# ScalarE's Softplus and Erf in place of exp, log, a polynomial and tanh in a feed-forward kernel

## Chip, cores and metric

The kernel runs on one core of a Trainium2 chip (trn2). The time is that of the device, in microseconds (us), from the core's start to its end; several executions are made and their median is given. Lower is better.

## What is computed

Two blocks follow each other. The first is attention between 512 tokens and 32 states of each of 8 heads, in both directions, for 8 batches; the second is a feed-forward block over all 8 * 544 = 4352 resulting rows, with an activation that is the input times the error function of its softplus:

```python
# x (8, 8, 512, 64), state (8, 8, 32, 64); softmax over the last axis, scale = 1/8
xread = softmax(scale * x @ state.T) @ state          # 512 rows per head
sread = softmax(scale * state @ x.T) @ x              # 32 rows per head
rows = concatenate([xread, sread], axis=2)            # -> (8 * 544, 512)
h = rows @ w_in                                       # w_in (512, 2048)
sp = maximum(h, 0) + log1p(exp(-abs(h)))              # softplus
out = (h * erf(sp)) @ w_out                           # w_out (2048, 512)
```

The two weights arrive as float64 and are made into float32 on the core.

## The kernel before

**Chunks and groups.** The feed-forward block goes over nine chunks of rows: one for the 512 token rows of each of the eight batches, and one for the 256 state rows of all batches together. A chunk is worked in four groups `g`; a group is four tiles of 128 hidden features. For each group `hidden` (line 239) makes the product with `w_in` (line 246: per tile four products over the 512 inputs, each run by TensorE as two MATMUL instructions on float32) into an accumulator tile `h` of PSUM, of which there are two (pool `ps_h`). ScalarE copies each tile into `hs` (line 248). The activation then runs over the whole group at once, 128 x 2048 elements for a chunk of 512 rows: VectorE cuts h at 3.95 (256), ScalarE takes exp (257), GpSimd adds one (258), ScalarE takes the logarithm (259), GpSimd makes the rounding's remainder in two steps (260, 261), VectorE subtracts it (262), ScalarE squares (263), VectorE runs a polynomial of degree 8 (264, six instructions at 267, 269), ScalarE takes tanh (271) and VectorE multiplies by `hs` (272). The result `gT` is the stationary operand of `project` (line 275), whose products with `w_out` (278) add up in four PSUM accumulators over the four groups. After the last group `store` copies them out on ScalarE (286) and SyncE's queue sends them to memory.

**Order.** The loop calls `hidden` of group g, then `project` of group g-1 (held back in `pending`), and after every odd group one of the two `attention` calls for the next batch. So between the hidden products of group g-1 and the projection of g-1 TensorE has the hidden products of group g to do. The four compute engines run their own queues in order; a planner that works from estimated durations makes those orders from the program, which is why the transposes of an attention stand between hidden products in the trace.

**Attention** (line 148) has a front part on TensorE: transposes of the state and of x (153, 161), and the two score products (169, 190). Then VectorE and ScalarE make the two softmaxes (175 to 202; exp on ScalarE at 179 and 198). The back part on TensorE is the transposes of the two results (206, 213), the products with the state (221) and with x (229). ScalarE copies each intermediate result out of PSUM. Two attentions run before the first chunk, and two during each of the first seven chunks.

**Weights.** During the first chunk each group first loads its two pieces of `w_in` and two of `w_out` (`weights`, line 134). A piece arrives as float64 bits in a buffer of the name `hs` (line 109; two buffers, shared with the `hs` of `hidden`), and seven instructions of VectorE (115 to 128; the last of them writes the weight tile) make it float32.

**Buffers** of the pool `act` (`hs`, `u`, `s`, `gT`) are two each; `w` is one.

Of the kernel before, what the change touches and what calls it, by code (L numbers as in the profile page):

```python
# [8 lines left out]
F32 = mybir.dt.float32  # L9
U32 = mybir.dt.uint32  # L10
ALU = mybir.AluOpType
ACTF = mybir.ActivationFunctionType
AX = mybir.AxisListType
PSUM = bass.MemoryType.PSUM

# erf(s) = tanh(s * P(s^2)) on 0 <= s <= 3.97, P of degree 8: its relative error is 3e-8, half a
# unit of fp32's last place. Above that erf is 1 in fp32; softplus(H_ONE) = 3.969, so h is cut there
# before it is made into s (and not where it multiplies the erf).
H_ONE = 3.95
ERF_P = [  # L20
    1.1283792021879724,
    0.10277131634542137,
    -0.0002021555576414212,
    -0.0006036769380557052,
    7.648746087340316e-05,
    -1.8604810636552222e-06,
    -5.151776104349058e-07,
    5.392234410610488e-08,
    -1.6409115403957545e-09,
]  # L30


@with_exitstack
def kernel(
# [8 lines left out]
    nc = tc.nc  # L43
    B, H, S, D = x.shape
    Ns = state.shape[2]
    d_model, d_ff = moe_w_in.shape
    P = 128
# [26 lines left out]

    # Rows (head of four, n), columns (head of the pair, d): each head's state in its own half, so
    # that a pair of heads is one product.
    st = const.tile([P, NH, B, 2 * D], F32, name="st")
# [3 lines left out]

    # Row p holds the tokens 4p .. 4p+3 of each head.
    def load_x(b, hb):
# [17 lines left out]
    def weight(dst, src, shape):  # L101
        """A piece of a weight. The bits of a float64 are made into a float32 here, rounded to
        the nearest."""
        if src.dtype == F32:
            nc.sync.dma_start(out=dst, in_=src)
            return
        i = shape[1]
        n = shape[0] * i
        raw = act.tile([P, 2 * n], U32, name="hs")
        nc.sync.dma_start(out=raw.rearrange("p (o i) -> p o i", i=2 * i), in_=src.bitcast(U32))  # L110
        words = raw.rearrange("p (n w) -> p n w", w=2)
        lo, hi = words[:, :, 0], words[:, :, 1]
        # 2^exponent with the sign: float32's bias is 896 less; what is too small becomes 0.
        e = act.tile([P, n], U32, name="u")
        nc.vector.tensor_scalar(e, hi, 20, 0x7FF, op0=ALU.logical_shift_right,
                                op1=ALU.bitwise_and)
        nc.vector.tensor_scalar(e, e, -896.0, 0.0, op0=ALU.add, op1=ALU.max)
        nc.vector.tensor_scalar(e, e, 255.0, 8388608.0, op0=ALU.min, op1=ALU.mult)
        nc.vector.scalar_tensor_tensor(out=e, in0=hi, scalar=0x80000000, in1=e,
                                       op0=ALU.bitwise_and, op1=ALU.bitwise_or)  # L120
        # The significand's upper 21 bits, and with the lower 32 behind the point.
        m = act.tile([P, n], U32, name="s")
        nc.vector.tensor_scalar(m, hi, 0xFFFFF, 0x100000, op0=ALU.bitwise_and,
                                op1=ALU.bitwise_or)
        f = act1.tile([P, n], F32, name="w")
        nc.vector.scalar_tensor_tensor(out=f, in0=lo, scalar=2.0 ** -32, in1=m,
                                       op0=ALU.mult, op1=ALU.add)
        nc.vector.scalar_tensor_tensor(  # L128
            out=dst, in0=f.rearrange("p (o i) -> p o i", i=i), scalar=2.0 ** -20,
            in1=e.bitcast(F32).rearrange("p (o i) -> p o i", i=i), op0=ALU.mult, op1=ALU.mult)  # L130
# [13 lines left out]

    # The state's own rows of the second part, features on the partitions, for all batches.
    sT = const.tile([P, NK, B, Ns], F32, name="sT")

    def attention(b, hb, xx):
        """Four heads of a batch: their rows of xx [feature, pair, token] and of sT."""
        xt = x_t.pop((b, hb))  # L150
# [13 lines left out]

        # Each token over the states.
        s1 = ps_at.tile([P, NC, QH, Ns], F32, name="at")
# [19 lines left out]

        # Each state over the tokens.
        s2 = ps_at.tile([P, S], F32, name="at")
# [35 lines left out]

        # Of each pair's product the blocks of one head with itself.
        sr = ps_at.tile([P, 2, 2 * Ns], F32, name="at")
# [8 lines left out]

    lead = ERF_P[-1]
    cs = [c / lead for c in ERF_P]

    def hidden(xx, n, g):
        """h * erf(softplus(h)) for four tiles of the hidden features, [feature, tile, token]."""  # L240
        hs = act.tile([P, GF, S], F32, name="hs")[:, :, 0:n]
        for i in range(GF):
            f0 = P * (GF * g + i)
            hp = ps_h.tile([P, S], F32, name="h")
            for k in range(NK):
                nc.tensor.matmul(out=hp[:, 0:n], lhsT=w_in[:, k, f0:f0 + P], rhs=xx[:, k, :],  # L246
                                 start=(k == 0), stop=(k == NK - 1))
            nc.scalar.copy(hs[:, i, :], hp[:, 0:n])  # L248

        # s = log1p(u) with u = exp(h): ln(w) - ((w - 1) - u), where w is 1 + u as it was rounded  # L250
        # and what follows it is exact, which keeps the small ones.
        u = act.tile([P, GF, S], F32, name="u")[:, :, 0:n]
        s = act.tile([P, GF, S], F32, name="s")[:, :, 0:n]
        w = act1.tile([P, GF, S], F32, name="w")[:, :, 0:n]
        gT = act.tile([P, GF, S], F32, name="gT")[:, :, 0:n]
        nc.vector.tensor_scalar(u, hs, H_ONE, None, op0=ALU.min)  # L256
        nc.scalar.activation(out=u, in_=u, func=ACTF.Exp)  # L257
        nc.gpsimd.tensor_scalar(w, u, 1.0, 1.0, op0=ALU.add, op1=ALU.mult)  # L258
        nc.scalar.activation(out=s, in_=w, func=ACTF.Ln)  # L259
        nc.gpsimd.tensor_scalar(w, w, -1.0, 1.0, op0=ALU.add, op1=ALU.mult)  # L260
        nc.gpsimd.tensor_tensor(w, w, u, op=ALU.subtract)  # L261
        nc.vector.tensor_tensor(s, s, w, op=ALU.subtract)  # L262
        nc.scalar.activation(out=u, in_=s, func=ACTF.Square)  # L263
        nc.vector.scalar_tensor_tensor(out=gT, in0=u, scalar=cs[-2], in1=u,  # L264
                                       op0=ALU.add, op1=ALU.mult)
        for c in cs[-3:0:-1]:
            nc.vector.scalar_tensor_tensor(out=gT, in0=gT, scalar=c, in1=u,  # L267
                                           op0=ALU.add, op1=ALU.mult)
        nc.vector.scalar_tensor_tensor(out=gT, in0=gT, scalar=cs[0], in1=s,  # L269
                                       op0=ALU.add, op1=ALU.mult)  # L270
        nc.scalar.activation(out=gT, in_=gT, func=ACTF.Tanh, scale=lead)  # L271
        nc.vector.tensor_tensor(gT, gT, hs, op=ALU.mult)  # L272
        return gT
# [90 lines left out]
```

## Time and profile before

| | |
|---|---|
| median of 3 runs | 1462.73 us (1460.02 to 1465.14) |
| span of the profiled execution, first to last instruction | 1459.6 us |
| TensorE (PE) busy | 1153.4 us, 79% |
| VectorE (DVE) busy | 1054.3 us, 72% |
| ScalarE (ACT) busy | 531.0 us, 36% |
| GpSimd (POOL) busy | 296.5 us, 20% |
| mean granted clock of TensorE | 0.889 of full speed |

The profile is of one execution on the chip. Its page lists, engine by engine, the busy time; the chain of work that ended last, followed back from the last instruction; and the groups of instructions with their idle time ahead of them and what ended that idle time. Ends of matmuls are modelled, so times between the starts of TensorE's instructions are more telling than the durations of single ones. "PEld" is TensorE's loading of the stationary operand, which runs beside the products. The granted clock is TensorE's, as a share of its full 2.4 GHz.

### The profile page before, as it was taken

What the parts mean: (1) busy time and instruction counts of PE and PEld (TensorE: products, weight loads), DVE (VectorE), ACT (ScalarE), POOL (GpSimd) and SP (SyncE); (2) the same over time, 40 slices, a digit from 0 to 9 for tenths busy, and PEclk for the clock granted to TensorE, in tenths of its full rate; (3) what the DMA queues carried; (4) which work ended last, traced back from release to release, by engine and by line L of the source; (5) the groups of instructions that cost most, each with busy time, mean ns of one, the idle gap of its engine ahead of it and who ended that gap; (6) DMA issues with size and microseconds to landing.
All of it is one profiled execution on the core that took longest, in us unless ns stands there. A gap on an engine that the chain in (4) does not pass through costs nothing.

```text
span 1459.6 us, 8120 instructions
## 1 busy us (share of the span) xinstructions
PE 1153.4 (79%) x3152; PEld 558.7 (38%) x3152; DVE 1054.3 (72%) x685; ACT 531.0 (36%) x587; POOL 296.5 (20%) x114
## 2 busy tenths in 40 slices
PE   6758575979897996979697969797897969694964
PEld 4434232434343443434343434343443424242541
DVE  2897988695758569495939585776858593859673
ACT  2323231434243343443344243434243334333432
POOL 0012020403222222222222221303022222222121
PEclk9968787979797998989798989999898979897987
DMA  4312221000000000000010001000000000000000
GB/s 129 101 44 86 88 71 58 15 29 0 15 0 29 15 1 11 33 0 15 0 44 0 15 0 29 15 15 0 0 29 0 0 0 29 0 0 0 29 0 15
DMA packets 45350, 35.13 MB, mean 24 GB/s; under 512 B 36864, under 2 KB 36864, under 8 KB 45312
## 3 DMA queue, kind: packets, MB, share of 16 engines
q1 hardware_dynamic: 45312, 34.61, 7.8%
q8 instruction: 25, 0.41, 0.1%
q14 instruction: 13, 0.11, 0.0%
HBM read 25.69 MB, written 8.91 MB: 24 GB/s over the span
## 4 chain that ended last, share of the span: by engine, by line
DVE 39%; PE 29%; ACT 16%; POOL 13%; issue 2%; DMA 0%; SPq 0%; POOLq 0%; ACTq 0%
DVE gT L267 18%; PE o L278 15%; PE h L246 9%; POOL w L261 7%; DVE gT L272 5%; ACT s L259 4%; ACT u L257 4%; POOL w L258 4%; DVE s L262 4%; DVE gT L264 3%; POOL w L260 3%; DVE u L256 3%; ACT u L263 3%; ACT gT L271 2%; PE at L229 2%
## 5 line engine op out<-in xcount | busy, mean ns | idle before, releaser
L278 PE MATMUL o<-w_out,gT 128*128 128x512 f32 x1088 | 510.9, 630 | 189.9 <-DVE gT L272 189.7
L246 PE MATMUL h<-xx,w_in 128*128 128x512 f32 x1024 | 467.9, 610 | 53.1 <-DVE w_in L128 52.8
L267 DVE SCALAR_TENSOR_TENSOR gT<-gT,u 128x2048 f32<-128x2048 f32 (+1 forms) x216 | 479.2, 2219 | 5.9
L278 PEld LDWEIGHTS o<-w_out,gT 128*128 128x128 f32 x1088 | 218.4, 203 | 477.7 <-issue 268.1
L246 PEld LDWEIGHTS h<-xx,w_in 128*128 128x128 f32 x1024 | 196.1, 196 | 294.4 <-issue 236.3
L258 POOL TENSOR_SCALAR w<-u 128x2048 f32<-128x2048 f32 (+1 forms) x36 | 66.4, 1845 | 1057.2 <-ACT u L257 1057.2
L262 DVE TENSOR_TENSOR s<-s,w 128x2048 f32<-128x2048 f32 (+1 forms) x36 | 78.1, 2169 | 222.8 <-POOL w L261 222.8
L248 ACT COPY hs<-h 128x512 f32<-128x512 f32 (+1 forms) x144 | 79.1, 560 | 293.3 <-PE h L246 243.9
L261 POOL TENSOR_TENSOR w<-w,u 128x2048 f32<-128x2048 f32 (+1 forms) x36 | 162.6, 4518 | 3.0
L272 DVE TENSOR_TENSOR gT<-gT,hs 128x2048 f32<-128x2048 f32 (+1 forms) x36 | 109.8, 3051 | 56.4 <-ACT gT L271 56.4
L263 ACT ACTIVATE u<-s 128x2048 f32<-128x2048 f32 (+1 forms) x36 | 65.4, 1815 | 161.5 <-DVE s L262 161.5
L264 DVE SCALAR_TENSOR_TENSOR gT<-u 128x2048 f32<-128x2048 f32 (+1 forms) x36 | 78.2, 2172 | 36.3 <-ACT u L263 36.0
L271 ACT ACTIVATE gT<-gT 128x2048 f32<-128x2048 f32 (+1 forms) x36 | 65.4, 1816 | 106.4 <-DVE gT L269 106.3
L269 DVE SCALAR_TENSOR_TENSOR gT<-gT,s 128x2048 f32<-128x2048 f32 (+1 forms) x36 | 101.8, 2827 | 0.7
L257 ACT ACTIVATE u<-u 128x2048 f32<-128x2048 f32 (+1 forms) x36 | 65.4, 1816 | 60.3 <-DVE u L256 60.3
L260 POOL TENSOR_SCALAR w<-w 128x2048 f32<-128x2048 f32 (+1 forms) x36 | 66.8, 1854 | 72.9 <-ACT s L259 72.9
L259 ACT ACTIVATE s<-w 128x2048 f32<-128x2048 f32 (+1 forms) x36 | 65.4, 1815 | 20.7 <-POOL w L258 20.6
L256 DVE TENSOR_SCALAR u<-hs 128x2048 f32<-128x2048 f32 (+1 forms) x36 | 41.9, 1163 | 32.6 <-ACT hs L248 32.6
L209 ACT COPY aT<-at 128x512 f32<-128x512 f32 x16 | 9.4, 584 | 121.3 <-PE at L206 121.2
L259 ACT ACT_TABLE_LOAD x36 | 46.2, 1283 | 0.6
L169 PE MATMUL at<-stT,xT 128*128 128x64 f32 x256 | 39.5, 305 | 7.8 <-ACT xT L163 7.4
L229 PEld LDWEIGHTS at<-a2T,x 128*128 128x128 f32 x256 | 36.4, 226 | 23.1 <-ACT xx L223 22.6
(55 smaller groups left out, 617.6 us busy)
## 6 DMA issues: line engine op xcount, KB each, us to landing
x<-in_x_dram SPq DMA_DIRECT2D x64, 128.0 KB, 2.9
hs<-in_moe_w_in_dram SPq DMA_DIRECT2D x8, 1024.0 KB, 5.2
hs<-in_moe_w_out_dram SPq DMA_DIRECT2D x8, 1024.0 KB, 4.8
out_dram<-ot SPq DMA_DIRECT2D x32, 256.0 KB, 2.2
st<-in_state_dram SPq DMA_DIRECT2D x8, 64.0 KB, 2.2
out_dram<-ot SPq DMA_DIRECT2D x8, 64.0 KB, 1.7
```

The costliest lines, as they stand in the source:

```text
L246: nc.tensor.matmul(out=hp[:, 0:n], lhsT=w_in[:, k, f0:f0 + P], rhs=xx[:, k, :], start=(k == 0), stop=(k == NK - 1))
L257: nc.scalar.activation(out=u, in_=u, func=ACTF.Exp)
L258: nc.gpsimd.tensor_scalar(w, u, 1.0, 1.0, op0=ALU.add, op1=ALU.mult)
L259: nc.scalar.activation(out=s, in_=w, func=ACTF.Ln)
L260: nc.gpsimd.tensor_scalar(w, w, -1.0, 1.0, op0=ALU.add, op1=ALU.mult)
L261: nc.gpsimd.tensor_tensor(w, w, u, op=ALU.subtract)
L262: nc.vector.tensor_tensor(s, s, w, op=ALU.subtract)
L263: nc.scalar.activation(out=u, in_=s, func=ACTF.Square)
L264: nc.vector.scalar_tensor_tensor(out=gT, in0=u, scalar=cs[-2], in1=u, op0=ALU.add, op1=ALU.mult)
L267: nc.vector.scalar_tensor_tensor(out=gT, in0=gT, scalar=c, in1=u, op0=ALU.add, op1=ALU.mult)
L272: nc.vector.tensor_tensor(gT, gT, hs, op=ALU.mult)
L278: nc.tensor.matmul(out=acc[r], lhsT=gT[:, i, P * r:P * r + P], rhs=w_out[:, GF * g + i, :], start=(g == 0 and i == 0), stop=(g == NG - 1 a ...
```

## The change

Each tile of h is now read from its accumulator by two engines: ScalarE's Softplus writes `s`, and VectorE's copy writes `hs`. When the four tiles of a group are there, one Erf of ScalarE runs over all of them in place, and VectorE multiplies by `hs`. The cut at 3.95, exp, logarithm, the three GpSimd instructions, the square, the polynomial and tanh are gone, with their constants; nothing is left for GpSimd in the loop. Everything outside `hidden` is as it was (comments fell away, so line numbers move).

```diff
     def hidden(xx, n, g):
         hs = act.tile([P, GF, S], F32, name="hs")[:, :, 0:n]
+        s = act.tile([P, GF, S], F32, name="s")[:, :, 0:n]
+        gT = act.tile([P, GF, S], F32, name="gT")[:, :, 0:n]
         for i in range(GF):
             f0 = P * (GF * g + i)
             hp = ps_h.tile([P, S], F32, name="h")
             for k in range(NK):
                 nc.tensor.matmul(out=hp[:, 0:n], lhsT=w_in[:, k, f0:f0 + P], rhs=xx[:, k, :],
                                  start=(k == 0), stop=(k == NK - 1))
-            nc.scalar.copy(hs[:, i, :], hp[:, 0:n])
-
-        u = act.tile([P, GF, S], F32, name="u")[:, :, 0:n]
-        s = act.tile([P, GF, S], F32, name="s")[:, :, 0:n]
-        w = act1.tile([P, GF, S], F32, name="w")[:, :, 0:n]
-        gT = act.tile([P, GF, S], F32, name="gT")[:, :, 0:n]
-        nc.vector.tensor_scalar(u, hs, H_ONE, None, op0=ALU.min)
-        nc.scalar.activation(out=u, in_=u, func=ACTF.Exp)
-        nc.gpsimd.tensor_scalar(w, u, 1.0, 1.0, op0=ALU.add, op1=ALU.mult)
-        nc.scalar.activation(out=s, in_=w, func=ACTF.Ln)
-        nc.gpsimd.tensor_scalar(w, w, -1.0, 1.0, op0=ALU.add, op1=ALU.mult)
-        nc.gpsimd.tensor_tensor(w, w, u, op=ALU.subtract)
-        nc.vector.tensor_tensor(s, s, w, op=ALU.subtract)
-        nc.scalar.activation(out=u, in_=s, func=ACTF.Square)
-        nc.vector.scalar_tensor_tensor(out=gT, in0=u, scalar=cs[-2], in1=u,
-                                       op0=ALU.add, op1=ALU.mult)
-        for c in cs[-3:0:-1]:
-            nc.vector.scalar_tensor_tensor(out=gT, in0=gT, scalar=c, in1=u,
-                                           op0=ALU.add, op1=ALU.mult)
-        nc.vector.scalar_tensor_tensor(out=gT, in0=gT, scalar=cs[0], in1=s,
-                                       op0=ALU.add, op1=ALU.mult)
-        nc.scalar.activation(out=gT, in_=gT, func=ACTF.Tanh, scale=lead)
-        nc.vector.tensor_tensor(gT, gT, hs, op=ALU.mult)
+            nc.scalar.activation(out=s[:, i, :], in_=hp[:, 0:n], func=ACTF.Softplus)
+            nc.vector.tensor_copy(hs[:, i, :], hp[:, 0:n])
+        nc.scalar.activation(out=s, in_=s, func=ACTF.Erf)
+        nc.vector.tensor_tensor(gT, s, hs, op=ALU.mult)
         return gT
```

## Rows read from the trace of the kernel before

**Rows 1.** The page's part 1: busy time (share of the span) and number of instructions
```profile
PE 1153.4 (79%) x3152; PEld 558.7 (38%) x3152; DVE 1054.3 (72%) x685; ACT 531.0 (36%) x587; POOL 296.5 (20%) x114
```

**Rows 2.** The page's part 4: the chain that ended last, by engine and line
```profile
DVE 39%; PE 29%; ACT 16%; POOL 13%; issue 2%; DMA 0%; SPq 0%; POOLq 0%; ACTq 0%
DVE gT L267 18%; PE o L278 15%; PE h L246 9%; POOL w L261 7%; DVE gT L272 5%; ACT s L259 4%; ACT u L257 4%; POOL w L258 4%; DVE s L262 4%; DVE gT L264 3%; POOL w L260 3%; DVE u L256 3%; ACT u L263 3%; ACT gT L271 2%; PE at L229 2%
```

**Rows 3.** Costliest groups, shapes merged: busy, mean ns of one | idle before, releaser
```profile
L278 PE MATMUL o<-w_out,gT 128*128 128x512 f32 x1088 | 510.9, 630 | 189.9 <-DVE gT L272 189.7
L246 PE MATMUL h<-xx,w_in 128*128 128x512 f32 x1024 | 467.9, 610 | 53.1 <-DVE w_in L128 52.8
L267 DVE SCALAR_TENSOR_TENSOR gT<-gT,u 128x2048 f32<-128x2048 f32 (+1 forms) x216 | 479.2, 2219 | 5.9
...
L248 ACT COPY hs<-h 128x512 f32<-128x512 f32 (+1 forms) x144 | 79.1, 560 | 293.3 <-PE h L246 243.9
```

**Rows 4.** TensorE's timeline, two groups and one attention: start, us, instructions [idle before]
```profile
731.25 0.60 PE L206 MATMUL at<-ident,a 128*128 128x128 f32 x4
...
732.53 1.61 PE L221 MATMUL at<-aT,st 64*128 64x512 f32 x4 [0.24 <-ACT aT L209]
734.32 2.00 PE L229 MATMUL at<-a2T,x 128*128 128x64 f32 x16 [0.19 <-ACT xx L223]
736.16 10.52 PE L246 MATMUL h<-xx,w_in 128*128 128x512 f32 x24
...
760.25 13.90 PE L246 MATMUL h<-xx,w_in 128*128 128x512 f32 x32
773.98 0.27 PE L153 MATMUL at<-ident,st 128*128 128x128 f32 x1
...
779.52 5.42 PE L246 MATMUL h<-xx,w_in 128*128 128x512 f32 x12
795.03 15.96 PE L278 MATMUL o<-w_out,gT 128*128 128x512 f32 x32 [10.09 <-DVE gT L272]
```

**Rows 5.** By windows: length, each engine's busy us, granted clock, DMA
```profile
773.50:779.50 6.00, 6.00 (x35) 3.78 (x33) 5.93 (x4) 3.11 (x5) 0.00 (x0) 1.00 0.00 1
...
784.90:795.00 10.10, 0.04 (x1) 0.00 (x0) 8.39 (x6) 5.74 (x6) 6.40 (x2) 0.69 0.00 0
795.00:799.00 4.00, 3.97 (x5) 1.85 (x6) 4.00 (x8) 2.81 (x3) 0.00 (x0) 0.50 0.00 0
```

**Rows 6.** All engines' timeline, 705 to 741 us
```profile
705.65 1.28 ACT L271 ACT_TABLE_LOAD   x1
...
706.94 1.91 ACT L271 ACTIVATE gT<-gT 128x2048 f32<-128x2048 f32 x1
...
708.89 5.46 DVE L272 TENSOR_TENSOR gT<-gT,hs 128x2048 f32<-128x2048 f32 x1 [1.67 <-ACT gT L271]
...
740.56 2.29 DVE L272 TENSOR_TENSOR gT<-gT,hs 128x2048 f32<-128x2048 f32 x1 [3.40 <-ACT gT L271]
```

**Rows 7.** Groups with shapes apart: attention's reads of PSUM and its exp
```profile
L177 DVE TENSOR_TENSOR a<-at,m 128x512 f32<-128x512 f32 x16 | 10.9, 681 | 0.1
...
L198 ACT ACTIVATE a<-at,m 128x512 f32<-128x512 f32 x16 | 10.8, 677 | 7.2 <-DVE m L195 7.2
...
L179 ACT ACTIVATE a<-a 128x512 f32<-128x512 f32 x16 | 9.9, 618 | 12.7 <-DVE a L177 12.7
```

**Rows 8.** VectorE's timeline: first and last of one weight piece's seven instructions
```profile
56.36 0.69 DVE L115 TENSOR_SCALAR u<-hs 128x1024 uint32<-128x1024 uint32 x1 [1.99 <-DMA hs<-in_moe_w_out_dram]
...
61.28 1.22 DVE L128 SCALAR_TENSOR_TENSOR w_out<-w,u 128x1024 f32<-128x1024 f32 x1
```

**Rows 9.** The page's part 6, DMA issues: KB each, us to landing
```profile
hs<-in_moe_w_in_dram SPq DMA_DIRECT2D x8, 1024.0 KB, 5.2
```

**Rows 10.** TensorE's timeline: the first hidden products of the kernel
```profile
48.91 4.94 PE L246 MATMUL h<-xx,w_in 128*128 128x512 f32 x8
```

**Rows 11.** Line 286 alone: copies out of the accumulators, first and last start
```profile
L286 ACT COPY ot<-o x34: 565/585/587, 309.0 to 1455.1; 128x512 f32<-128x512 f32 x34
```

More of the change, by code (lines that the diff above doesn't have):

```diff
@@ L14 @@
 PSUM = bass.MemoryType.PSUM
[L19 to L30, printed above, removed]
 @with_exitstack
@@ L234, in attention @@
                            sr[D * e:D * e + D, :, Ns * e:Ns * e + Ns])
-    lead = ERF_P[-1]
-    cs = [c / lead for c in ERF_P]
     def hidden(xx, n, g):
         hs = act.tile([P, GF, S], F32, name="hs")[:, :, 0:n]
+        s = act.tile([P, GF, S], F32, name="s")[:, :, 0:n]
+        gT = act.tile([P, GF, S], F32, name="gT")[:, :, 0:n]
         for i in range(GF):
```

## Prediction, made before the changed kernel was run

> **What bounds the kernel now.** I read the busy times first: TensorE 79%, VectorE 72%, no engine full [rows 1]. So no engine's rate is the whole bound, and the chain that ended last is next: 39% of it is VectorE, 29% TensorE, 16% ScalarE, 13% GpSimd, and under VectorE, ScalarE and GpSimd nearly every line is one of the activation's [rows 2]. The chain runs through the activation and only at times through products. Third, who makes TensorE wait: 189.7 us in front of the projection for gT (272), 52.8 us in front of hidden products for a converted weight piece (128) [rows 3]. TensorE's timeline shows the pattern: hidden products, the front of an attention, more hidden products, then a hole of 10.09 us until gT arrives [rows 4]. The hole costs twice: the granted clock falls in it, and the first 4 us behind it run at 0.50, the level of 1.2 GHz [rows 5].
>
> What TensorE needs without holes: 32 hidden products take from 760.25 to 773.98, so 13.73 us or 0.429 us each; a projection of 32 has the same form and I give it the same rate. The front of an attention lies between 773.98 and 779.52 with four hidden products among it: 5.54 - 4 * 0.429 = 3.82 us; its back from 731.25 to 736.16: 4.91 us [rows 4]. In that front the clock stays at 1.00 [rows 5], so small products don't slow the stream.
>
> **The change, part by part.**
>
> Removed: per group on VectorE the cut, the subtraction, and the eight polynomial instructions (six of them at 2.2 us, 479.2 us in all [rows 3]), GpSimd's three (all but a few of its 296.5 us [rows 1]), and on ScalarE Exp, Ln, Square and Tanh, for which one Erf comes. In its place the latency from the last hidden product to gT is a last Softplus, a table load, Erf, the multiply.
>
> Added: Softplus per tile in place of the copy. No row shows it. Below stands the copy from PSUM, 0.56 us mean; above, the two functions that softplus was made of, each with a load of its own: 2 * (0.62 + 1.28) = 3.8 us [rows 3, 6, 7]. I take 0.6, because Exp from PSUM (0.68 with a bias operand) and Exp in SBUF (0.62) are near the copy [rows 7]: on this engine the function has hardly mattered. Erf over 2048 columns: Tanh's 1.91 us [rows 6]; bounds are that and twice that, were it two passes. VectorE's copy from PSUM: 0.68 us like the subtraction that reads PSUM [rows 7]; four per group are 2.7 us where 20 us and more went away. The multiply: 2.29 us, its time alone, in place of 5.46 us beside GpSimd's work [rows 6].
>
> Table loads: a load took 1.28 us and Tanh started at its end, 705.65 + 1.28 = 706.93 against 706.94 [rows 6]. If Softplus, Erf and attention's Exp each want their own, two groups and an attention need six, perhaps eight: 10.2 us of ScalarE. ScalarE for that stretch: 8 * 0.6 + 2 * 1.91 + 10.2, and some 7 us for attention and stores, makes 26 us, against TensorE's 2 * 27.46 + 8.73 = 63.7 us. The loads hide under the products, as long as an accumulator comes free in time: two of them, and a tile's products take 8 * 0.429 = 3.43 us, so a Softplus may be some 3.4 us late before TensorE feels it.
>
> The Trainium skill, page "ScalarE: Activation LUTs", section "What ACT_TABLE_LOAD costs", puts a drain of about 1.38 us beside the load, some 2.66 us for a switch, and tells authors to batch by set, which speaks against this change, with its three sets. Rows 6 show no such drain ahead of Tanh. By the page the eight switches would be an estimated 21 us of ScalarE in place of 10; ScalarE would stand at 37 of 63.7 us and the sum would stay.
>
> Latency of gT: 0.6 + 1.28 + 1.91 + 2.29 and 0.2 for hand-offs is 6.3 us, and TensorE has the projection of the group before (13.7 us) in that time. So the holes go. What is late next is TensorE itself.
>
> First chunk: here VectorE still converts the weights. One piece takes from 56.36 to 62.50, 6.1 us [rows 8], and its load 5.2 us [rows 9]. Four pieces per group are 24.6 us of VectorE, with copies and multiply 29.6 us, near TensorE's 27.5 + 4.4 us. The pieces share two buffers with hs; while hs holds one, pieces come one by one, at 5.2 + 6.1 = 11.3 us. I followed buffers through the second group: its first w_in piece is done at about 71 us, the second at 83, hs gets a buffer at about 88, hidden products end near 96; then about 31 us per group, and the four hidden products end near 160, where TensorE alone would need till 145. So 15 us of holes stay here; bounds 0 (everything covered) and 45 us (half of the waits that stand behind lines 128 and 272 in that chunk now).
>
> **The sum.** Until the first hidden products: 48.9 us, unchanged [rows 10]. Hidden products: 1024 * 0.429 = 439.3; the 128 of half length at half that, 27.5. Projections: 1088 * 0.429 = 466.8. Fourteen attentions at 8.73: 122.2. From the last product's copy to the end: 1459.6 - 1455.1 = 4.5 [rows 11]. Together 1109 us. To it: cold start of the first hidden products (4.94 us for 8 where 3.43 would do) 1.5; first chunk 15; low clock behind some four holes there, 2 us each (a projection behind a hole took 795.03 to 810.82, 15.79 against 13.73 [rows 4]), 8; half a microsecond per attention where TensorE waits for a copy, 7. That is 1140.5 us against the span of 1459.6. The median of before lies 3.1 us above that span; with the same on top I predict 1143 us, 22% less.
>
> **The rivals.**
>
> Attention uncovered: in its softmax TensorE has only what the planner put there. If nothing, TensorE waits for max, subtract, load, Exp, sum, reciprocal and multiply: 3 to 4 VectorE steps of 0.7, 1.28, 0.62 and the small ones, some 5.5 us, and 2 at low clock: 14 * 7.5 = 105, 1248 us. For it: two Exps and new table loads stand in ScalarE's queue between the Softplus of neighbouring groups. Against: hidden products stand between the attention's parts in the trace [rows 4].
>
> Late accumulators: a Softplus that waits or takes 3.8 us, above a tile's 3.43, stops TensorE at 0.4 us per tile, 144 times: 1143 + 58 = 1200 us. That would also be the change that doesn't do what it says: a Softplus made of two passes. By the page's 2.66 us, two switches and a Softplus per tile would be an estimated 5.9 us, 2.5 over, which would bring the time near 1500; that needs Softplus and another set to alternate tile by tile, and Erf comes once per four; I give it 0.01 of this rival's chance.
>
> Slower than before: the planner, with the activation now short, puts the projection of a group right behind that group's own hidden products. Then TensorE waits out gT's latency each time, 6.3 us and 2.1 for the clock, 8.4 * 36 = 302: 1445 us. It gets slower than before from 8.9 us per group on; with the two Exps of an attention and their load ahead in ScalarE's queue (1.28 + 0.62 + 0.68) it is 11, so 1143 + 396 = 1539 us. For it: order on the queues follows estimated times. Against: every projection of before in the rows read stands behind the next group's hidden products, and the program asks for that order.
>
> **How the numbers follow.** Forecast (1104 to 1190, first chunk and copies at their bounds) 0.74; attention uncovered 0.11; late accumulators 0.08; projection uncovered, part or whole, 0.07, of which 0.04 end slower and 0.01 within 0.3%, what a measurement of this kernel can tell from no change. The low end, 1104 us, is the bare 1109 + 3 us and 8 less, should other products fill the waits for ScalarE's copies inside an attention (0.24 and 0.19 us of its 8.73 [rows 4], fourteen times) and a little at the end. The high end 1225 takes in late accumulators and a part of the attention rival; beyond lie about 0.15. Faster 0.95, same 0.01, slower 0.04.
>
> **What would show it.** TensorE's share above 90%, granted clock about 0.95; no wait of the projection for line 272's successor beyond the first chunk; 63 to 65 us between the attentions of one chunk; GpSimd idle; table loads of 1.28 us, some 100 of them; Softplus at 0.6 us; first copy out of an accumulator near 190 us in place of 309 [rows 11]. Wrong would be: waits of hidden products for Softplus or the copy in every group, a hole behind each front of attention, or first-chunk groups beyond 40 us.

## The result, and the profile after

The changed kernel takes 1125.61 us (median of four runs, 1122.53 to 1126.09), the kernel before 1462.33 beside it: a ratio of 0.769, with a 95% interval of 0.767 to 0.771. The forecast was 1143 us, 17 us above. The profiled execution took 1126.09 us; its span is 1124.3.

The page's part 1 (busy time, share of the span, instructions) and the chain that ended last by engine, as in [rows 1, 2]:

```profile
PE 1084.4 (96%) x3152; PEld 530.1 (47%) x3152; DVE 334.7 (30%) x469; ACT 365.4 (33%) x494; POOL 0.7 (0%) x6
...
PE 94%; DVE 2%; ACT 2%; DMA 1%; SPq 0%; issue 0%; ACTq 0%
PE h L230 42%; PE o L241 41%; PE at L212 3%; PE at L152 3%; PE at L204 2%; PE at L144 2%; PE at L173 1%; ACT xx L206 1%; PE at L196 1%; PE at L189 1%; DMA hs<-in_moe_w_in_dram 0%; ACT s L234 0%; DVE u L102 0%; ACT L234 0%; SPq L69 0%
```

TensorE now is the chain: 94% of it, where the activation's engines had 68%. The costliest groups say the same in their idle column (busy, mean ns of one | idle before, releaser), beside [rows 3]:

```profile
L241 PE MATMUL o<-w_out,gT 128*128 128x512 f32 x1088 | 477.6, 592 | 0.7 <-DVE gT L235 0.7
L230 PE MATMUL h<-xx,w_in 128*128 128x512 f32 x1024 | 460.1, 600 | 6.7 <-DVE w_in L111 6.6
...
L232 ACT ACTIVATE s<-h 128x512 f32<-128x512 f32 (+1 forms) x144 | 82.2, 573 | 403.9 <-PE h L230 403.5
...
L234 ACT ACTIVATE s<-s 128x2048 f32<-128x2048 f32 (+1 forms) x36 | 65.3, 1815 | 0.4
L232 ACT ACT_TABLE_LOAD x37 | 47.5, 1283 | 42.1 <-DVE w L109 41.5
...
L234 ACT ACT_TABLE_LOAD x36 | 46.2, 1283 | 0.6
```

189.7 us of waiting for gT became 0.7, and 52.8 us for weight pieces became 6.6. Softplus takes 0.573 us in the mean, about what the copy took that it replaces; Erf costs what Tanh cost.

What stands between a group's last hidden product and its gT is plain in the timeline of all engines (start, us, engine and line [idle before]), in place of [rows 6]:

```profile
536.55 8.75 PE L241 MATMUL o<-w_out,gT 128*128 128x512 f32 x20
...
536.75 0.60 ACT L232 ACTIVATE s<-h 128x512 f32<-128x512 f32 x1 [2.84 <-PE h L230]
...
537.36 1.28 ACT L234 ACT_TABLE_LOAD   x1
537.38 0.69 DVE L233 COPY hs<-h 128x512 f32<-128x512 f32 x1 [2.74 <-ACT s L232]
...
538.65 1.91 ACT L234 ACTIVATE s<-s 128x2048 f32<-128x2048 f32 x1
...
540.60 2.29 DVE L235 TENSOR_TENSOR gT<-s,hs 128x2048 f32<-128x2048 f32 x1 [2.53 <-ACT s L234]
```

Hidden products end at 536.55, gT is there at 540.60 + 2.29 = 542.89: 6.3 us. TensorE alone over one period of two groups and an attention, in place of [rows 4]:

```profile
536.55 13.90 PE L241 MATMUL o<-w_out,gT 128*128 128x512 f32 x32
550.28 0.27 PE L136 MATMUL at<-ident,st 128*128 128x128 f32 x1
...
555.09 2.84 PE L230 MATMUL h<-xx,w_in 128*128 128x512 f32 x6
557.77 2.74 PE L241 MATMUL o<-w_out,gT 128*128 128x512 f32 x6
560.35 0.60 PE L189 MATMUL at<-ident,a 128*128 128x128 f32 x4
...
586.46 13.90 PE L230 MATMUL h<-xx,w_in 128*128 128x512 f32 x32
600.20 13.90 PE L241 MATMUL o<-w_out,gT 128*128 128x512 f32 x32
613.93 0.27 PE L136 MATMUL at<-ident,st 128*128 128x128 f32 x1
```

No hole for gT is left; the longest wait in the period is 0.67 us, at 563.97, for a copy of the attention (line 206). During the softmax (554 to 560) TensorE has six hidden products and six of a projection. The period is 613.93 - 550.28 = 63.65 us; less four times 13.73 the attention costs 8.7 us.

By windows (length, busy us of PE, PEld, DVE, ACT, POOL, granted clock, DMA share, GB/s), beside [rows 5]: from 80 us to the end the granted clock is 1.00, its 2.4 GHz level.

```profile
0.00:80.00 80.00, 56.17 (x181) 33.52 (x182) 49.60 (x77) 24.36 (x40) 0.70 (x6) 0.79 0.43 124
80.00:1124.30 1044.30, 1028.23 (x2972) 496.57 (x2970) 285.12 (x393) 341.04 (x454) 0.00 (x0) 1.00 0.08 24
```

The copies out of the accumulators, first and last start, beside [rows 11], divide the gain:

```profile
L249 ACT COPY ot<-o x34: 567/586/587, 180.4 to 1119.8; 128x512 f32<-128x512 f32 x34
```

The first copy comes 309.0 - 180.4 = 128.6 us earlier, and from first to last it takes 939.4 us in place of 1146.1, 206.7 less.

### The profile page after: what moved, and what is told of

Same layout as the page of the kernel before. It is cut to its first block, busy times and chain, and to the rows that moved or that the text cites. A ratio compares the mean times of both kernels' runs of the same rounds, so it can differ in the third digit from the quotient of the medians.

```text
span 1124.3 us, 7665 instructions
## 1 busy us (share of the span) xinstructions
PE 1084.4 (96%) x3152; PEld 530.1 (47%) x3152; DVE 334.7 (30%) x469; ACT 365.4 (33%) x494; POOL 0.7 (0%) x6
## 4 chain that ended last, share of the span: by engine, by line
PE 94%; DVE 2%; ACT 2%; DMA 1%; SPq 0%; issue 0%; ACTq 0%
PE h L230 42%; PE o L241 41%; PE at L212 3%; PE at L152 3%; PE at L204 2%; PE at L144 2%; PE at L173 1%; ACT xx L206 1%; PE at L196 1%; PE at L189 1%; DMA hs<-in_moe_w_in_dram 0%; ACT s L234 0%; DVE u L102 0%; ACT L234 0%; SPq L69 0%
## 5 line engine op out<-in xcount | busy, mean ns | idle before, releaser
L241 PE MATMUL o<-w_out,gT 128*128 128x512 f32 x1088 | 477.6, 592 | 0.7 <-DVE gT L235 0.7
L233 DVE COPY hs<-h 128x512 f32<-128x512 f32 (+1 forms) x144 | 95.2, 661 | 518.0 <-ACT s L232 518.0
L232 ACT ACTIVATE s<-h 128x512 f32<-128x512 f32 (+1 forms) x144 | 82.2, 573 | 403.9 <-PE h L230 403.5
L235 DVE TENSOR_TENSOR gT<-s,hs 128x2048 f32<-128x2048 f32 (+1 forms) x36 | 78.2, 2173 | 78.6 <-ACT s L234 78.6
L234 ACT ACTIVATE s<-s 128x2048 f32<-128x2048 f32 (+1 forms) x36 | 65.3, 1815 | 0.4
L212 PE MATMUL at<-a2T,x 128*128 128x64 f32 x256 | 33.6, 287 | 9.2 <-ACT xx L206 9.2
L212 PEld LDWEIGHTS at<-a2T,x 128*128 128x128 f32 x256 | 31.4, 200 | 23.4 <-ACT xx L206 23.4
L152 PEld LDWEIGHTS at<-stT,xT 128*128 128x128 f32 x256 | 34.3, 209 | 8.3 <-ACT xT L146 5.4
L230 PE MATMUL h<-sT,w_in 128*128 128x256 f32 x128 | 28.9, 379 | 0.0
L230 PEld LDWEIGHTS h<-sT,w_in 128*128 128x128 f32 x128 | 24.3, 190 | 6.7 <-issue 3.8
L204 PE MATMUL at<-aT,st 64*128 64x512 f32 x64 | 21.5, 694 | 0.9 <-ACT aT L192 0.9
```

The costliest lines, as they stand in the source:

```text
L152: nc.tensor.matmul(out=s1[:, c, 2 * j:2 * j + 2, :], lhsT=xT[:, j, P * c:P * c + P], rhs=stT[:, 2 * Ns * j:2 * Ns * j + 2 * Ns], start=Tru ...
L204: nc.tensor.matmul(out=y, lhsT=st[rows, hb, b, :], rhs=aT[rows, :], start=True, stop=True)
L212: nc.tensor.matmul(out=sr[:, j, :], lhsT=xt[:, c, 2 * j:2 * j + 2, :], rhs=a2T[:, c, 2 * Ns * j:2 * Ns * j + 2 * Ns], start=(c == 0), stop ...
L232: nc.scalar.activation(out=s[:, i, :], in_=hp[:, 0:n], func=ACTF.Softplus)
L233: nc.vector.tensor_copy(hs[:, i, :], hp[:, 0:n])
L234: nc.scalar.activation(out=s, in_=s, func=ACTF.Erf)
```

## The experiments

The theory: what counted in the kernel before was the length of the way from a group's hidden products to its gT, against the work TensorE has between hidden products and projection. That work is called the cover here. For one group of before the way was 48 us: its hidden products end at 736.16 + 24 * 0.429 = 746.5 and its multiply ends at 794.97. TensorE, with a projection, 48 hidden products and the front of an attention between, came to its projection 38 us behind them and waited 10.09 [rows 4]. Now the way is 6.3 us, and the cover is 21.2 us at the end of a chunk (536.55 to 557.77 above); in the same trace it is 22.3, 36.2 and 27.5 us for the other three groups of the chunks 1 to 6. The theory is about the 206.7 us behind the first copy; in the first chunk VectorE's weight pieces and the buffers hs come into it as well. Rivals: ScalarE's table loads or late accumulators set the pace; or reading the accumulator directly is itself the gain.

**Softplus alone.** The polynomial and Tanh of before come back behind the new Softplus (without the cut at 3.95).

```diff
-        nc.scalar.activation(out=s, in_=s, func=ACTF.Erf)
-        nc.vector.tensor_tensor(gT, s, hs, op=ALU.mult)
+        nc.scalar.activation(out=u, in_=s, func=ACTF.Square)
+        ... eight scalar_tensor_tensor on VectorE, as before
+        nc.scalar.activation(out=gT, in_=gT, func=ACTF.Tanh, scale=lead)
+        nc.vector.tensor_tensor(gT, gT, hs, op=ALU.mult)
```

> Half of the change: ScalarE's Softplus from the accumulator, then the square, the polynomial of degree 8 and tanh of before (the cut at 3.95 is left out). The way from a group's last hidden product to gT is then 0.6 + 1.9 + 8 * 2.29 + 1.3 + 1.9 + 2.29 = 26.3 us. Theory A (only the length of that way counts: TensorE has the projection of the group before the last and the next hidden products in that time, 2 * 13.73 = 27.5 us, and the rest is free): hardly a hole outside the first chunk; in the first chunk VectorE has 24.6 us of weights and 23 us of activation per group, some 50 us against 32, so about 70 us more there: 1196 us, range 1150 to 1230. Rival B (what counts is VectorE's load, and the gain goes with the part of it that was removed): VectorE keeps 661 of the 779 us of removed work, so most of the gain is lost: about 1400 us.

Measured: 1263.25 us, ratio 0.863 (0.861 to 0.865). Above the theory's range, and far below the rival's 1400. TensorE's waits (in total, times, longest):

```profile
PE h L242 <- DVE w_in L123: 42.1, 4, 13.8
PE o L264 <- DVE gT L258: 25.2, 8, 5.1
PE at L201 <- DVE a L179: 19.4, 7, 4.5
```

The first copy stands at 271.3, 91 us behind the changed kernel's: VectorE has the weight pieces there (24.6 us a group by the prediction's count) and eight polynomial steps of 2.29 us again, more than TensorE's 27.5. Behind the first copy it loses 47 us, which is the larger part of the miss: the expectation had 70 us for the first chunk and next to nothing behind it. There gT is late seven times, 24.2 us in all. Three of these are chunk ends: gT comes 26.2 us behind its hidden products, as was reckoned, but TensorE is at the projection after 21.3 us and waits 4.9. The softmax, whose steps stand between polynomial steps on VectorE, makes TensorE wait another 16.2 us.

**Erf alone.** Copy, Exp, Ln and GpSimd's three instructions as before, then Erf.

```diff
-            nc.scalar.activation(out=s[:, i, :], in_=hp[:, 0:n], func=ACTF.Softplus)
-            nc.vector.tensor_copy(hs[:, i, :], hp[:, 0:n])
+            nc.scalar.copy(hs[:, i, :], hp[:, 0:n])
+        ... min, Exp, + 1, Ln, - 1, two subtractions, as before
         nc.scalar.activation(out=s, in_=s, func=ACTF.Erf)
```

> The other half: softplus by exp, GpSimd and logarithm as before, with the cut and the copy to hs on ScalarE, and Erf in place of the polynomial and tanh. The way to gT is 1.2 + 1.3 + 1.9 + 1.9 + 1.9 + 1.9 + 4.5 + 2.3 + 1.3 + 1.9 + 2.3 = 22.4 us, under the 27.5 us that TensorE has. Theory A (length of the way against that slack): no holes outside the first chunk, there hs is held some 16 us longer per group, so up to 50 us more: 1150 us, range 1126 to 1190; together with the other half alone the two gains would add up to far more than the whole. Rival B (gain by removed load): polynomial is 661 of 779 us of VectorE's removed work: about 1175 us; Rival C (each engine of the long chain that is left makes waits): above 1200 us. A and B are near each other here, the other half tells them apart.

Measured: 1192.45 us, 0.815 (0.813 to 0.817), just above the range. The first copy is at 242.8, 62 us later than in the changed kernel; from there to the last it takes 944.6 us, 5 more than 939.4. So behind the first chunk Erf alone gives nearly everything. GpSimd's work is all still there (286.3 us busy), so there that work as such was not what held the kernel before. Its waits:

```profile
PE at L189 <- DVE z L183: 19.0, 3, 8.1
PE at L189 <- DVE a L167: 13.8, 1, 13.8
PE o L249 <- DVE gT L243: 12.9, 7, 5.5
```

Behind the first chunk gT is 1.2 us late once a chunk, 21.1 us behind its hidden products where the cover is 19.9. The rival that goes by removed load is near this time (1175) but far from the other half's (1400 against 1263).

Each half alone brings most of the gain: 1462 - 1263 = 199 us and 1462 - 1192 = 270, together 469 where the whole brings 337. Gains that overlap like this are what a threshold would give: once the way is short enough, the rest of it is worth little. By themselves they don't show it; the runs with a later gT below test it. In the first chunk the halves bring 38 and 66 us of the 128.6; how much of that is VectorE's freed time and how much the earlier release of hs, no run separates.

**ScalarE's load raised by table switches.** Erf moves into the loop over tiles, so that Softplus and Erf alternate.

```diff
-        nc.scalar.activation(out=s, in_=s, func=ACTF.Erf)
+            nc.scalar.activation(out=s[:, i, :], in_=s[:, i, :], func=ACTF.Erf)
```

> The changed kernel with Erf behind each tile's Softplus in place of one Erf over four tiles, so that two table sets alternate tile by tile: 288 loads and more in place of 87. By the rows a tile then takes ScalarE 0.6 + 1.28 + 0.65 + 1.28 = 3.8 us, four tiles 15.2 us, of 27.5 us per group: if the two accumulators and the projection in between absorb it, 1126 us within 10 us. The prediction's rival of late accumulators, 0.4 us for each of 144 tiles: 1185 us. With a drain of 1.38 us at each load, which the Trainium skill states (ScalarE: Activation LUTs, What ACT_TABLE_LOAD costs) and no row here shows, a tile would take an estimated 6.6 us and a group 26 us of ScalarE: with attention above what it has, an estimated 1200 us and more.

Measured: 1122.39 us, 0.767 (0.765 to 0.769); not slower. The groups of loads on the two lines (by the page, 37 and 36 in the changed kernel):

```profile
L232 ACT ACT_TABLE_LOAD x129 | 165.5, 1283 | 32.8 <-DVE w L109 30.5
...
L234 ACT ACT_TABLE_LOAD x129 | 165.5, 1283 | 2.3
```

ScalarE's timeline there (start, us):

```profile
507.03 0.63 ACT L234 ACTIVATE s<-s 128x512 f32<-128x512 f32 x1
...
507.68 1.28 ACT L232 ACT_TABLE_LOAD   x1
508.97 0.60 ACT L232 ACTIVATE s<-h 128x512 f32<-128x512 f32 x1
509.59 1.28 ACT L234 ACT_TABLE_LOAD   x1
```

ScalarE is busy 626.3 us in place of 365.4, and the time does not rise. A switch costs 1.28 us: the load starts 0.02 us after the Erf before it and Softplus 0.01 us after the load. The Trainium skill ("ScalarE: Activation LUTs", "What ACT_TABLE_LOAD costs") puts a drain of about 1.38 us on top; these rows show none. The rival of late accumulators, at a switch pair and both functions per tile (3.8 us against a tile's 3.43), falls too, and with it its price: the prediction charged each tile the 0.4 us by which ScalarE is slower, but ScalarE catches up while TensorE does the projection, another 13.7 us per group (before the first tile at 524.90 it idles 12.09 us).

**Softplus not from the accumulator.**

```diff
-            nc.scalar.activation(out=s[:, i, :], in_=hp[:, 0:n], func=ACTF.Softplus)
-            nc.vector.tensor_copy(hs[:, i, :], hp[:, 0:n])
+            nc.scalar.copy(hs[:, i, :], hp[:, 0:n])
+        nc.scalar.activation(out=s, in_=hs, func=ACTF.Softplus)
```

> The changed kernel without VectorE's copy and without the read of the accumulator by Softplus: ScalarE copies each tile to hs as before, and one Softplus runs over the four tiles from there. The way to gT grows by a load and a Softplus over 2048 columns less one over 512, some 2.6 us. Theory A: no difference that can be measured, 1126 us within 6 us, since both ways stay under the slack and each accumulator comes free within a tile's 3.43 us. Rival: reading the accumulator directly is worth something of itself, then slower by 2.6 us per group, 1126 + 94 = 1220 us.

Measured: 1127.06 us, 0.771 (0.770 to 0.772), as the theory had it. From first to last copy it takes 939.4 us, as the changed kernel does; in the first chunk one hole of 8.6 us for gT stands where that has one of 6.65 for a weight piece. So reading the accumulator directly is worth nothing here. What Softplus saves over the chain of Exp, Ln and GpSimd, some 65 us against the run with Erf alone, lies nearly all in the first chunk.

**No lag.** Each group's projection is called right after its own hidden products.

```diff
             gT = hidden(cur, n, g)
-            if pending is not None:
-                pending()
...
+            pending()
             if b + 1 < B and g % 2 == 1:
```

> The changed kernel with each group's projection asked for right behind that group's own hidden products, without the lag of one group that the program had. If the program's order were what TensorE runs (the slower rival of the prediction), it would wait 6.3 us and lose 2.1 us of clock at each of 36 groups: 1126 + 302 = about 1430 us. If the planner fills the way to gT with the next group's hidden products by itself: 1126 us, within 10 us.

Measured: 1204.38 us, 0.822 (0.818 to 0.826): neither. TensorE waits for gT only 8.8 us in all, since the planner puts hidden products of the next group between; the order that the rival needs didn't come about. The time goes at the end of each chunk, where the last attention needs its softmax and no projection is left to cover it. TensorE's timeline there:

```profile
588.62 14.00 PE L241 MATMUL o<-w_out,gT 128*128 128x512 f32 x32
...
603.56 0.66 PE L189 MATMUL at<-ident,a 128*128 128x128 f32 x4
606.57 1.09 PE L196 MATMUL at<-ident,a 128*128 128x128 f32 x4 [2.36 <-DVE a L185]
...
610.34 3.68 PE L212 MATMUL at<-a2T,x 128*128 128x64 f32 x16
```

From 602.5 to 613.8 the granted clock is 0.67, and L212's sixteen products take 3.47 us up to the next start where they took 1.84 in the changed kernel (563.97 to 565.81). The wait ahead of L196 comes seven times, 14.6 us in all. From first to last copy the kernel loses 1009.6 - 939.4 = 70 us. One chunk takes 136.5 us (from the start of one attention, line 136, at 482.24 to the next but one at 618.73) where the changed kernel takes 2 * 63.65 = 127.3, so 9.2 us per chunk.

**gT later, on GpSimd.** Nine or fourteen multiplications by one behind the multiply, in chunks 1 to 7.

```diff
         nc.vector.tensor_tensor(gT, s, hs, op=ALU.mult)
+        for _ in range(9 if late else 0):      # 14 in the second
+            nc.gpsimd.tensor_scalar(gT, gT, 1.0, 1.0, op0=ALU.mult, op1=ALU.mult)
```

> The changed kernel with gT made later in the chunks 1 to 7: nine multiplications by one on GpSimd, which is idle in the changed kernel, behind the multiply, 9 * 1.9 = 17 us. The way to gT is then 6.3 + 17.3 = 23.6 us, still under the 27.5 us that the projection of the group before and the next hidden products take. Theory A (that slack): 1126 us, within 12 us. Rival B (length of the way costs as it is, in each group): 28 * 17.3 = 484 us more, 1610 us; or in part, clearly above 1140.

> The same with fourteen multiplications on GpSimd, 14 * 1.9 = 27 us: the way to gT is 33.2 us, 5.7 us over the 27.5 us of a group without an attention behind it and under the 36 us of a group with one. Theory A: holes of some 5.7 us, with 2 us of low clock behind each, in the groups without an attention, 16 of them: up to 123 us more, less where the planner finds other products to put there: 1150 to 1250 us. Where holes stay away even so, or the 17 us run already had them, the slack is not what theory A says.

Measured: 1175.65 us, 0.804 (0.803 to 0.805) with nine; 1318.12, 0.900 (0.896 to 0.904) with fourteen. Both above what was expected. With nine, gT itself is in time (3.9 us of waits in all); the loss is elsewhere. Two steps of the softmax on VectorE, by line:

```profile
L185 DVE TENSOR_SCALAR a<-a,z 128x512 f32<-128x512 f32 x16 | 24.5, 1533 | 0.0
...
L165 DVE TENSOR_SCALAR z<-z 128x16 f32<-128x16 f32 x16 | 18.3, 1147 | 0.0
```

And in the changed kernel:

```profile
L185 DVE TENSOR_SCALAR a<-a,z 128x512 f32<-128x512 f32 x16 | 7.0, 440 | 0.0
...
L165 DVE TENSOR_SCALAR z<-z 128x16 f32<-128x16 f32 x16 | 2.7, 166 | 0.0
```

Beside GpSimd these two take 3.5 and 7 times as long, about 1 us more each, while the softmax's reductions (0.68 us) and its steps on 128x1 (0.15 us) keep their times; and so TensorE waits 29.5 us for the softmax (line 167). The Trainium skill ("SBUF — State Buffer", "Who interferes with whom") says that VectorE and GpSimd share one pair of ports, held by one at a time; the two stretched steps agree, each losing less than one of GpSimd's multiplications (1.9 us). As a test of latency alone the pair is spoilt; fourteen shows TensorE waiting for gT again, 14 times and 58.3 us, with this second loss on top.

**gT later, by transfers.** In chunks 1 to 7, gT goes three or five times between its buffer and that of s.

```diff
+            nc.vector.tensor_tensor(s, s, hs, op=ALU.mult)
+            for k in range(3):                 # 5 in the second
+                nc.sync.dma_start(out=s if k % 2 else gT, in_=gT if k % 2 else s)
```

> The delay of gT without GpSimd, whose work in the 17 us run stretched steps of attention on VectorE (0.17 to 1.45 us, 0.45 to 2.02 us): in the chunks 1 to 7 the product goes three times through the DMA engines, from s to gT, back to s and to gT again, before the projection may use it. A load of the same size took 5.2 us, so some 5 to 7 us per hop, 15 to 21 us in all, and the way to gT is 21 to 27 us. No engine has more to do. Theory A: TensorE gives it 27.5 us, but 21 us at the end of each chunk, where the changed kernel's trace has the last projection begin 21 us behind its hidden products (536.6 to 557.8 us): at 21 us in all 1126 us, within 6 us; at 27 us holes at 7 chunk ends only, of 6 us and 2 us of clock, 1180 us. Rival B (every microsecond of the way costs): 28 * 15 us and more, above 1500 us.

> The same with five hops, 25 to 35 us: the way to gT is 31 to 41 us, beyond the 27.5 us. Theory A: now each group without an attention behind it has a hole of the difference, 4 to 14 us, with 2 us of clock, and the chunk ends of 10 to 20 us: at hops of 5 us 16 * 6 + 7 * 12 = 180 us more, 1306 us; at hops of 7 us 16 * 16 + 7 * 22 = 410 us more, 1536 us. That the step from three hops to five costs ten times and more what the first three cost is what tells a threshold from a price per microsecond.

Measured: with three 1126.7 us, 0.769 (0.767 to 0.771), as expected; with five 1180.88, 0.807 (0.804 to 0.809), far less than expected. The transfers of the run with three, issue to landing:

```profile
gT<-s SPq DMA_DIRECT2D x56, 1024.0 KB, 4.6
s<-gT SPq DMA_DIRECT2D x28, 1024.0 KB, 4.5
```

So 6.3 us became about 20, just under the least cover of 21.2, and cost nothing, with no engine slowed. With five, the way goes from 529.18 to about 558.4 (the last is issued at 553.83), 29 us. TensorE's timeline there:

```profile
529.18 13.90 PE L246 MATMUL o<-w_out,gT 128*128 128x512 f32 x32
542.91 13.90 PE L230 MATMUL h<-xx,w_in 128*128 128x512 f32 x32
...
557.19 1.02 PE L230 MATMUL h<-xx,w_in 128*128 128x512 f32 x2
...
560.21 13.90 PE L246 MATMUL o<-w_out,gT 128*128 128x512 f32 x32
...
580.60 1.09 PE L189 MATMUL at<-ident,a 128*128 128x128 f32 x4 [2.70 <-DVE a L167]
```

The planner puts the start of the attention and six hidden products ahead of the projection (556.65 to 560.21), so that gT still is in time. In the chunks 2 to 6 its projections begin 31.0 to 38.2 us behind their hidden products. What is lost is the projection as cover of the softmax: six such holes, 16.2 us in all, and the lower clock behind them. From 580.6 to 590.0 it is 0.50, so about 4.7 us are lost; with the hole of 2.70 that is most of the some 8 us by which a chunk is longer here. So three hops show that a longer way is free below the cover. Five hops don't show holes for gT above it, since the order changed; they show what avoiding these holes costs.

**The weights of the first group ahead.** All of its weight pieces ahead of the first two attentions, or those of w_in alone.

```diff
+    weights(0)                                 # weights_in(0) in the second
     xx = new_xx()
...
             if b == 0:
-                weights(g)
+                if g > 0:
+                    weights(g)                 # in the second weights_out(0) stays here
```

> A version meant to beat both kernels: the changed kernel with the first group's weights loaded and converted ahead of the first two attentions in the program, so that VectorE's conversions fall into the time in which it waited for TensorE. What is left outside the steady stretch of the changed kernel is TensorE's start: holes of 2.7 and 5.3 us before the first hidden products, one of 6.65 us for a weight piece, and low clock behind them. If theory A is right that only TensorE's work and its start are left: 5 to 14 us less, 1112 to 1121 us. If the conversions delay the attentions' own steps on VectorE: as the changed kernel or slower, 1126 to 1135 us.

> A version meant to beat both kernels, after the one with all of the first group's weights ahead was slower (VectorE converted the w_out pieces ahead of the second attention's softmax, and TensorE had a hole of 10.28 us there): only the first two pieces of w_in are loaded and converted ahead of the two attentions. They are done at about 31 us, before that softmax. Then eight hidden products fill TensorE's hole of 5.3 us, and the hole of 6.65 us for the next group's piece shrinks: 4 to 12 us less than the changed kernel, 1114 to 1122 us. If pieces of w_out still come between the steps of the softmax: 1126 us or a little more.

Measured: all ahead 1134.03 us, 0.775 (0.772 to 0.777), slower than the changed kernel; w_in alone 1118.65, 0.765 (0.764 to 0.766), faster than it by some 0.6% (1117.99 to 1120.27 against 1122.53 to 1126.09, not run side by side), and faster than both kernels. The first, TensorE's timeline: a softmax stands behind w_out's conversions on VectorE.

```profile
50.44 1.08 PE L189 MATMUL at<-ident,a 128*128 128x128 f32 x4 [10.28 <-DVE z L183]
```

The changed kernel's start, for comparison, with its two holes of that stretch:

```profile
38.17 1.08 PE L189 MATMUL at<-ident,a 128*128 128x128 f32 x4 [5.32 <-DVE z L184]
...
47.05 6.29 PE L230 MATMUL h<-xx,w_in 128*128 128x512 f32 x8
...
75.04 5.98 PE L230 MATMUL h<-xx,w_in 128*128 128x512 f32 x8 [6.65 <-DVE w_in L111]
```

And with w_in alone ahead: hidden products now stand in the second attention's softmax, and both holes shrink to under 1 us. Two others of 2.6 and 2.4 us open (at 93.78 and 132.17); from the second chunk on TensorE is 8.0 us ahead of the changed kernel.

```profile
33.08 4.93 PE L232 MATMUL h<-xx,w_in 128*128 128x512 f32 x8
38.36 0.63 PE L191 MATMUL at<-ident,a 128*128 128x128 f32 x4 [0.35 <-DVE z L186]
...
60.86 3.70 PE L232 MATMUL h<-xx,w_in 128*128 128x512 f32 x8 [0.91 <-DVE w_in L111]
```

## Why the prediction was right

**What bounds the kernel.** Right for the changed kernel: TensorE is 96% busy and 94% of the chain. With either half alone gT's waits behind the first copy are 24.2 and 12.9 us, where all waits for gT were 189.7 before.

**The products.** Right to the digit: 32 in 13.73 us, and 8.7 us per attention against 8.73.

**Latency of gT.** 6.3 us was forecast and measured, with Softplus 0.60 for a full tile, load 1.28, Erf 1.91, multiply 2.29. The step beside it was too small: it counted only the projection of the group before as cover. The three-hop run shows that 20 us are hidden, more than one projection's 13.7: the hidden products of the next group lie between as well, whole or in part, which makes the cover 21.2 to 36.2 us. The 27.5 us of the later expectations is one of its four values and not the least; Softplus alone missed its range partly by that. The slack was understated in the prediction; the result didn't hang on it.

**Table loads.** About 100 were forecast, 88 came, and they lie under products. Tripled to 275, they still do.

**What was mis-sized.** The terms that the forecast added by hand to the bare 1109 us. What the sum without these additions leaves of the span is 1124.3 - 4.5 - 47.05 - 1055.8 = 17.0 us (1055.8 is the products and the fourteen attentions); the forecast had 1.5 + 15 + 8 + 7 = 31.5 for it. Half a microsecond per attention (7 us) was counted twice: the waits for ScalarE's copies are there, 0.67 us in the period above, but inside the 8.73, as the period of 63.65 us shows. Of the first chunk one hole of 6.65 us is left, and the clock costs there: eight products at 47.05 took 6.13 us up to the next start and those at 75.04 took 5.82, where 3.43 would do, 5.1 us. Of the remaining 5 us, 2.9 are four waits of under 1 us in the first chunk; the rest I did not place. The upper bound of 45 us for that chunk was misread: in the kernel before, the waits for lines 128 and 272 there are 52.8 and 8.1 us, and half of that is 30. The start took 47.05 us, not 48.9, and that is luck: of nine other runs that begin alike, eight reach the first hidden product at 48.8 to 49.2 us and one at 47.3. Ahead of the span came 1.8 us in place of 3.1; the 3.1 sets a median against the span of another execution. Together -1.9 - 14.5 - 1.3 = -17.7: the unrounded 1143.8 becomes 1126.1, the profiled run's time.

**The signs.** TensorE is at 96%, the clock at 0.985 over the span, the first copy at 180.4 where near 190 was said, GpSimd idle: all as the forecast wanted.

**The rivals.** Attention uncovered: not in the changed kernel, but real; it is what the no-lag and five-hop runs lost at chunk ends (70 and 55 us). Its price of 7.5 us per attention is near the 9 and 8 us per chunk, but by luck: the hole is 2.4 to 2.7 us where 5.5 was priced, and the low clock behind it makes most of the rest, where 2 was priced. It falls on one attention of a chunk's two. Late accumulators: refuted by Erf in every tile. The projection right behind its own hidden products: the planner avoided it even where the program asked for it, so its price wasn't tested; forcing it on TensorE's queue wasn't tried.

## What to carry to other kernels

When a chain on slower engines runs beside a matrix engine, measure its length from last input to first use, and compare it with the least work that lies between on the matrix engine: above that, the excess shows as a wait (10.09 us where the way was 48 and the cover 38), unless a planner moves other work there and uncovers something else; below it, more shortening gives nothing, and the parts' gains don't add up. Busy shares don't tell this: VectorE at 75% with the polynomial and ScalarE at 56% with 275 table loads were 140 us apart. Once the chain is covered, look at the stretches without cover, here the start and the end of each chunk's softmax.

## What the hardware showed that was not expected

- VectorE's copy never ran beside Softplus of the same tile: it starts when Softplus ends (536.75 + 0.60 = 537.35, then 537.38), and the page puts 518.0 us of VectorE's idle time ahead of line 233 down to it; in all 144 tiles the two never overlap. Two readers of one accumulator cost 1.3 us one after the other, hidden here under a tile's 3.43. Whether the chip or the program's order does this the runs don't tell.
- Beside nine multiplications of GpSimd per group, VectorE's TENSOR_SCALAR over 128x16 went from 0.17 to 1.15 us in the mean and that over 128x512 from 0.44 to 1.53, while others kept their times (128x1: 0.15 us; the reductions: 0.68).
- A transfer of 1 MB within SBUF took 4.5 us from issue to landing, and 84 of them left the time unchanged (1126.7 against 1125.61 us).
